# Applying an adaLN modulation after the transpose, one scalar per partition, in a linear-attention and GeGLU block

## The chip, the core and the metric

The kernel runs on one core of a Trainium2 chip, in bf16 with float32 accumulation. The core has five engines that run side by side and wait for each other through semaphores: TensorE (PE), VectorE (DVE), ScalarE (ACT), GpSimd (POOL) and SyncE (SP); SP, ACT and POOL also issue DMA transfers, each from its own queue and in program order. The metric is the device time of one launch in microseconds (us), as a median over launches.

## What is computed

One transformer block with adaptive layer norm. A conditioning vector `c` gives six vectors of 1024 entries each (shift, scale and gate, once for each half), here called `sa, ca, ga, sb, cb, gb`:

```python
mod = (_silu(c) @ w_mod).reshape(c.shape[0], 6, 1, -1)
sa, ca, ga, sb, cb, gb = (mod[:, k] for k in range(6))      # shortened
h = _layernorm(x) * (1 + ca) + sa
x = x + ga * A(h, wqkv, wo)
h = _layernorm(x) * (1 + cb) + sb
x = x + gb * B(h, w_gate, w_up, w_down)
```

`x` is 2048 tokens by 1024. `A` is linear attention with 32 heads of 32: `q, k, v = h @ wqkv`, `phi(t) = where(t > 0, t + 1, exp(t)) + 1e-6`, `kv = phi(k)^T v` and `z = sum phi(k)` for each head, `o = phi(q) kv / (phi(q) z)`, then `o @ wo`. `B` is `(gelu(h @ w_gate) * (h @ w_up)) @ w_down` with an inner width of 3584. `w_mod` is 1024 by 6144.

## The kernel before

Tokens lie in 16 tiles of 128 partitions. The kernel is written as one program order; a tracker derives every semaphore wait from overlapping memory regions, and each engine then runs its own operations in that order. Its stages are: mod vectors and layer norm 1, k and v for 16 tiles, `z` and `kv`, then q with the normalisation and the `wo` projection, layer norm 2 of the first four tiles, and a feed-forward loop over four quarters of 512 tokens.

The mod vectors are needed along the free axis of a token-major tile, the same in all 128 partitions. So each half vector is a product of the broadcast `silu(c)` (`bc`, 128 equal columns for each of 8 blocks) with a panel of `w_mod` of 1 MB:

```python
def mod_group(pan, n, defer=False, dve_copy=False):
    b = next_bank()
    items = [(bank(b), bc[:, t, :], pan[:, t, :]) for t in range(NDT)]     # 8 matmuls, 128x512
    T.mm(items)
    ...                                          # one 128x512 eviction into modt[k6], by ACT or DVE

early_evacs = []
for n in (2, 3, 0, 1):                           # ca, sa
    k = load_panel(wmod_v[:, :, n * 512:(n + 1) * 512])                    # SP queue
    early_evacs.append(mod_group(panel[k], n, defer=True, dve_copy=(n in (0, 1))))

def kv_panel_loads():
    ...                                          # four load_panel of wqkv (k, v) into the same four slots
    for k in range(4):
        T.dma("sp", mpanel[k], wmod_v[:, :, (4 + k) * 512:(5 + k) * 512], d_mpanel[k])
```

Layer norm is a pipeline of stages over tiles. In each step, every stage works on its own tile, later stages first:

```python
def s_stats(): ...      # DVE: bn_stats x2
...                     # DVE: bn_aggr, + eps; POOL: pow(-0.5); DVE: -mean * rstd
def s_hn():    T.op("act", ... a.activation(hn, x_ap, AF.Identity, bias=nm, scale=rs) ...)
def s_mod1():  T.op("dve", ... v.tensor_tensor(h, hn, ca1_t, ALU.mult) ...)    # 128x1024
def s_mod2():  T.op("dve", ... v.tensor_tensor(h, h, sa_t, ALU.add) ...)       # 128x1024
def s_tr():    T.op("sp", ... e.dma_start_transpose(dest, h) ..., ctr=dsem, inc=16)
return [s_stats, s_aggr, s_eps, s_pow, s_nm, s_hn, s_mod1, s_mod2, s_tr]

for i in range(NST):
    stages = ln_stages(xring[i % NXR1], modt[CA1], modt[SA], hT[:, i, :, :], d_trh[i], h_t)
    items.append([None] + stages + [None, (lambda i=i: kv_groups(i))])
# hooks, called after a step of the pipeline:
#   2: kv_panel_loads   6: evictions of early_evacs   m = 6..15: load_x(m)
#   8: late_mod_a: four mod_group on mpanel, then the next four w_mod panels on the SP queue
#  14: late_mod_b: four mod_group on those
```

`kv_groups(i)` holds four groups of eight 128x512 matmuls and their evictions. After the pipeline come the `z` groups (32 matmuls 128x512), the `kv` groups (128 matmuls 128x128), and a loop over pairs of tiles:

```python
for p in range(npairs + 2):
    if p < npairs:
        er_a = q_groups_and_act(ta); er_b = q_groups_and_act(tb_)
        q_minadd(er_a); q_minadd(er_b); q_ttadd(er_a); q_ttadd(er_b)     # DVE
    if 1 <= p <= npairs:
        chain_pair(2 * (p - 1), 2 * (p - 1) + 1)       # DVE: the denominators, and the scaled phi(q)
    ...                                                # wo_proj; transposes by DMA of pair p-2; numT
    if p == npairs:
        ln2_0_build()
        run_pipeline([st_[:8] for st_ in ln2_0_items])
...                                                    # the last wo_proj
for st_ in ln2_0_items:
    st_[8]()                                           # transposes into hT2, on the SP queue
```

`hT2` lies at `BIG + 120 KB`, inside the region of `oT`, which the last `wo_proj` still reads. In the feed-forward loop each quarter runs the gate and up projections (28 blocks, 448 matmuls), whose last step on each block of `AT` is a DVE operation (line 745, for the last block line 749), and then the down projection (224 matmuls):

```python
for q in range(NSC):
    ...                                                # load_panel of w_gate, w_up; gate, up, gelu -> AT
    if q + 1 < NSC:
        nxt = ln2_items(q + 1)
        run_pipeline([st_[:8] for st_ in nxt])
        pendingF = [st_[8] for st_ in nxt]
    for jj in range(4):
        for dc in range(2):
            its = [(bank(b), AT[:, jf, jj * P:(jj + 1) * P], Wd[:, jf, dc * 512:(dc + 1) * 512]) for jf in range(NFT)]
            T.mm(its)                                  # one wait for all of AT, ahead of its 28 matmuls
        ...                                            # DVE: times gb, plus x1
        T.dma("pool", out2d[j * P:(j + 1) * P, :], stg, d_o[so % NXR])
        if pendingF: pendingF.pop(0)()                 # the transpose of tile jj of the next quarter
```

Of the kernel before, what the change touches and what calls it, by code (L numbers as in the profile page):

```python
# [13 lines left out]
P = 128  # L14
# [219 lines left out]

def _build(nc, stack, A_x, A_wqkv, A_wo, B_w_gate, B_w_up, B_w_down, c, w_mod, out):
# [28 lines left out]
    cT = view(768, [P, 8], BF16)  # L264
# [3 lines left out]
    negh = view(896, [P, 1], F32)  # L268
    NLNS = 6
    def ln_small(k):  # L270
        base = 1024 + (k % NLNS) * 64
        st = view(base, [P, 12], F32)
        mv = view(base + 48, [P, 2], F32)
        rs = view(base + 56, [P, 1], F32)
        nm = view(base + 60, [P, 1], F32)
        return st, mv, rs, nm
    vi = view(2048, [P, P], I32)
# [3 lines left out]
    def den_small(k):  # L281
# [4 lines left out]
    modt = [view(4 * KB + k * 2 * KB, [P, D], BF16) for k in range(6)]  # L286
    SA, CA1, GA, SB_, CB1, GB = range(6)
# [4 lines left out]
    NHN = 2  # L292
    NHH = 3
    NHHB = 4
    hn_t = [view(TEMPS + k * 2 * KB, [P, D], BF16) for k in range(NHN)]
    h_t = [view(TEMPS + 4 * KB + k * 2 * KB, [P, D], BF16) for k in range(NHH)]
    hB_t = [view(TEMPS + 4 * KB + k * 2 * KB, [P, D], BF16) for k in range(NHHB)]
    NE1 = 4
    e1_t = [view(TEMPS + 10 * KB + k * KB, [P, 512], BF16) for k in range(NE1)]
    bc = view(TEMPS + 18 * KB, [P, NDT, P], BF16)  # L300
    xring = [view(48 * KB + k * 2 * KB, [P, D], BF16) for k in range(4)] + \
            [view(TEMPS + 14 * KB + k * 2 * KB, [P, D], BF16) for k in range(2)]
    NXR1 = 6
# [8 lines left out]
    e2_t = [view(TEMPS + 16 * KB + k * KB, [P, 512], BF16) for k in range(NE2)]  # L312
    NGT = 2
    sqz_t = [view(TEMPS + 12 * KB + k * KB, [P, 512], BF16) for k in range(NGT)]
    th_t = [view(TEMPS + 14 * KB + k * KB, [P, 512], BF16) for k in range(NGT)]
    usb_t = [view(TEMPS + 16 * KB + k * KB, [P, 512], BF16) for k in range(NGT)]
# [11 lines left out]
    hn2a_t = [view(BIG + 64 * KB + k * 2 * KB, [P, D], BF16) for k in range(2)]  # L328
    h2a_t = [view(BIG + 64 * KB + (2 + k) * 2 * KB, [P, D], BF16) for k in range(4)]
    AT = view(BIG, [P, NFT, 512], BF16)  # L330
    Wd = view(BIG + 64 * KB, [P, NFT, D], BF16)
    hT2 = view(BIG + 120 * KB, [P, 4, NDT, P], BF16)
# [23 lines left out]
    T.op("pool", lambda g: g.iota(vi, [[1, P]], base=0, channel_multiplier=-1), W=[vi])  # L356
    T.op("dve", lambda v: v.tensor_scalar(ident, vi, 0.0, None, ALU.is_equal), R=[vi], W=[ident])
    T.op("pool", lambda g: g.iota(vm.rearrange("p (a b) -> p a b", a=4), [[DH, 4], [0, DH]], base=0, channel_multiplier=-1), W=[vm])
    T.op("dve", lambda v: v.tensor_scalar(t1m, vm, 0.0, None, ALU.is_le), R=[vm], W=[t1m])
    T.op("dve", lambda v: v.scalar_tensor_tensor(mask, vm, -float(DH - 1), t1m, ALU.is_ge, ALU.mult), R=[vm, t1m], W=[mask])  # L360
    T.op("pool", lambda g: g.memset(ones, 1.0), W=[ones])
    T.op("pool", lambda g: g.memset(negh, -0.5), W=[negh])

# [15 lines left out]
    c8 = t1m[0:NDT, :]  # L379
    T.dma("act", c8, c[0].rearrange("(t p) -> t p", p=P), d_c)  # L380

# [3 lines left out]

    for i in range(NXR1):
        load_x(i, NXR1)

    pc8 = bank_bf16(7)[:, 0:NDT]
# [4 lines left out]
    T.op("dve", lambda v: v.tensor_tensor(siluT, thc, cTf, ALU.mult), R=[thc, cTf], W=[siluT])  # L394
    T.op("dve", lambda v: v.tensor_tensor(bc, ones.unsqueeze(1).to_broadcast([P, NDT, P]),
                                          siluT.unsqueeze(2).to_broadcast([P, NDT, P]), ALU.mult),
         R=[ones, siluT], W=[bc])

    def mod_group(pan, n, defer=False, dve_copy=False):
        b = next_bank()  # L400
        items = [(bank(b), bc[:, t, :], pan[:, t, :]) for t in range(NDT)]
        T.mm(items)
        k6, half = n // 2, n % 2
        dst = modt[k6][:, half * 512:(half + 1) * 512]
        if k6 in (CA1, CB1):
            ev = lambda: T.op("act", lambda a: a.activation(dst, bank(b), AF.Identity, bias=1.0, scale=1.0), R=[bank(b)], W=[dst])
        elif dve_copy:
            ev = lambda: T.op("dve", lambda v: v.tensor_copy(dst, bank(b)), R=[bank(b)], W=[dst])
        else:
            ev = lambda: T.op("act", lambda a: a.activation(dst, bank(b), AF.Copy), R=[bank(b)], W=[dst])  # L410
        if defer:
            return ev
        ev()

    early_evacs = []
    for n in (2, 3, 0, 1):
        k = load_panel(wmod_v[:, :, n * 512:(n + 1) * 512])
        early_evacs.append(mod_group(panel[k], n, defer=True, dve_copy=(n in (0, 1))))
# [7 lines left out]
    def kv_panel_loads():  # L426
        a0 = load_panel(wqkv_v[:, :, 2 * 512:3 * 512])
        a1 = load_panel(wqkv_v[:, :, 3 * 512:4 * 512])
        a2 = load_panel(wqkv_v[:, :, 4 * 512:5 * 512])
        a3 = load_panel(wqkv_v[:, :, 5 * 512:6 * 512])  # L430
        assert (a0, a1, a2, a3) == (ks0, ks1, vs0, vs1)
        for k in range(4):
            T.dma("sp", mpanel[k], wmod_v[:, :, (4 + k) * 512:(5 + k) * 512], d_mpanel[k])
# [3 lines left out]
    def ln_stages(x_ap, ca1_t, sa_t, dest, dsem, hring, hnring=None):  # L437
# [3 lines left out]
        hnring = hn_t if hnring is None else hnring  # L441
        hn = hnring[kk % len(hnring)]
        h = hring[kk % len(hring)]
# [20 lines left out]
        def s_mod1():  # L464
            T.op("dve", lambda v: v.tensor_tensor(h, hn, ca1_t, ALU.mult), R=[hn, ca1_t], W=[h])  # L465

        def s_mod2():
            T.op("dve", lambda v: v.tensor_tensor(h, h, sa_t, ALU.add), R=[h, sa_t], W=[h])  # L468

        def s_tr():  # L470
            T.op("sp", lambda e: e.dma_start_transpose(dest, h), R=[h], W=[dest], ctr=dsem, inc=16)

        return [s_stats, s_aggr, s_eps, s_pow, s_nm, s_hn, s_mod1, s_mod2, s_tr]

    def run_pipeline(stage_lists, hooks=None):
        n = len(stage_lists)
        if n == 0:
            return
        ns = max(len(x) for x in stage_lists)
        for step in range(n + ns - 1):  # L480
            for s in reversed(range(ns)):
                i = step - s
                if 0 <= i < n and s < len(stage_lists[i]) and stage_lists[i][s] is not None:
                    stage_lists[i][s]()
            if hooks and step in hooks:
                hooks[step]()
# [27 lines left out]
    for i in range(NST):  # L514
        stages = ln_stages(xring[i % NXR1], modt[CA1], modt[SA], hT[:, i, :, :], d_trh[i], h_t)

        items.append([None] + stages + [None, (lambda i=i: kv_groups(i))])
    hooks = {}
    for m in range(NXR1, NST):
        hooks[m] = (lambda m=m: load_x(m, NXR1))  # L520
    def late_mod_a():
        for k in range(4):
            mod_group(mpanel[k], 4 + k)
        for k in range(4):
            T.dma("sp", mpanel[k], wmod_v[:, :, (8 + k) * 512:(9 + k) * 512], d_mpanel[k])
    def late_mod_b():
        for k in range(4):
            mod_group(mpanel[k], 8 + k)
    def early_evac_hook():
        for ev in early_evacs:  # L530
            ev()
    prev2 = hooks.get(2)
    hooks[2] = (lambda: (prev2() if prev2 else None, kv_panel_loads()))
    prev6 = hooks.get(6)
    hooks[6] = (lambda: (prev6() if prev6 else None, early_evac_hook()))
    prev8 = hooks.get(8)
    hooks[8] = (lambda: (prev8() if prev8 else None, late_mod_a()))
    prev14 = hooks.get(14)
    hooks[14] = (lambda: (prev14() if prev14 else None, late_mod_b()))
# [7 lines left out]
    assert len({q0, q1, wo0, wo1}) == 4, (q0, q1, wo0, wo1)  # L547
    for half in range(2):
        its = [(bank(half), ones, pk[:, i, half * 512:(half + 1) * 512]) for i in range(NST)]
        T.mm(its)  # L550
    for bb in range(2):
        its = []
        for i in range(NST):
            for cc in range(4):
                c_ = bb * 4 + cc
                its.append((ps[:, (2 + bb) * 512 + cc * P:(2 + bb) * 512 + (cc + 1) * P],
                            pk[:, i, c_ * P:(c_ + 1) * P], vv[:, i, c_ * P:(c_ + 1) * P]))
        T.mm(its, W=[bank(2 + bb)])
    for half in range(2):
        T.op("act", lambda a, half=half: a.activation(zbs[:, half * 512:(half + 1) * 512], bank(half), AF.Copy),  # L560
             R=[bank(half)], W=[zbs[:, half * 512:(half + 1) * 512]])
    for bb in range(2):
        src = bank(2 + bb).rearrange("p (a b) -> p a b", a=4)
        dstk = kvbd[:, bb * 4:(bb + 1) * 4, :]
        T.op("dve", lambda v, src=src, dstk=dstk, bb=bb: v.tensor_tensor(dstk, src, mask.unsqueeze(1).to_broadcast([P, 4, P]), ALU.mult),
             R=[bank(2 + bb), mask], W=[dstk])
# [67 lines left out]
    def wo_proj(q, jjs=(0, 1, 2, 3)):  # L634
        for jj in jjs:
# [11 lines left out]
            for (ysb, cols) in grs:  # L647
                dst = x1[:, j, cols]
# [165 lines left out]
```

## Time and profile before

| what | us |
|---|---|
| median of 4 launches | 953.18 (951.58 to 953.86) |
| span of the profiled launch | 949.8 |
| PE busy | 864.5 (91%) |
| DVE busy | 480.3 (51%) |
| ACT busy | 340.6 (36%) |
| POOL busy | 45.0 (5%) |

The span is divided by the stage: the first matmul on k and v starts at 59.58 us, the feed-forward loop at 347.75 us. In the profile a line such as L209 is the helper that records every matmul, so stages are told apart by time and by shape. "Idle before" is the time an engine stood still before an instruction, with the engine or transfer that ended it last.

### The profile page before, as it was taken

To read this page: it belongs to the slowest core of one execution; us is meant where nothing else is said; L and a number is where in the kernel's file an instruction comes from. 1 tells how busy PE (TensorE), PEld (TensorE's weight loads), DVE (VectorE), ACT (ScalarE), POOL (GpSimd) and SP (SyncE) were. 2 spreads that over 40 slices of the span, in tenths; PEclk is the share of its full clock that TensorE was granted. 3 is DMA by queue.
4 is the path that set the end of the run, shared out by engine and by line. 5 is a ranking of instruction groups with operands and counts; after the bars stand their busy time and mean duration, and the time that the engine had idled before them with its cause. 6 is when DMAs were issued, how large, how long until landed. Compare 5 with 4: busy or idle time off the path is not lost.

```text
span 949.8 us, 10474 instructions
## 1 busy us (share of the span) xinstructions
PE 864.5 (91%) x4001; PEld 389.0 (41%) x4001; DVE 480.3 (51%) x955; ACT 340.6 (36%) x574; POOL 45.0 (5%) x88
## 2 busy tenths in 40 slices
PE   4349999996998659998999999899999899999898
PEld 1124444452443224443444444344444344444343
DVE  5226555248779515556515555614555713555411
ACT  2024443244463514544104554203544402444300
POOL 3011010000000100000100000100000000000000
PEclk9779999998999779999999999999999999999999
DMA  9963132503133277770623531441452170543000
GB/s 323 350 192 86 34 78 45 177 1 67 45 89 67 55 220 236 242 248 18 182 73 101 174 126 54 100 155 57 131 178 89 27 218 23 177 144 123 1 23 23
DMA packets 137329, 112.88 MB, mean 119 GB/s; under 512 B 52800, under 2 KB 130624, under 8 KB 137280
## 3 DMA queue, kind: packets, MB, share of 16 engines
q1 hardware_dynamic: 133424, 99.63, 35.2%
q0 software_dynamic: 3840, 12.59, 4.0%
q8 instruction: 32, 0.52, 0.2%
q14 instruction: 17, 0.14, 0.0%
q10 hardware_dynamic: 16, 0.00, 0.0%
HBM read 95.42 MB, written 4.19 MB: 105 GB/s over the span
## 4 chain that ended last, share of the span: by engine, by line
PE 86%; DMA 4%; DVE 4%; issue 3%; ACT 2%; SPq 2%; POOL 0%; ACTq 0%; DVEq 0%; POOLq 0%
PE ps L209 86%; DMA arena<-in_w_mod_dram 3%; SPq L197 2%; ACT arena L632 1%; DMA arena<-in_B_w_gate_dram 1%; ACT arena L462 1%; DVE arena L600 0%; ACT arena L645 0%; DMA arena<-arena 0%; DVE arena L617 0%; DVE arena L590 0%; DVE arena L749 0%; ACT arena L738 0%; DVE arena L595 0%; DVE arena L447 0%
## 5 line engine op out<-in xcount | busy, mean ns | idle before, releaser
L209 PE MATMUL ps<-arena 128*128 128x512 bf16 (+1 forms) x4000 | 864.3, 379 | 73.0 <-DMA arena<-in_w_mod_dram 18.2
L209 PEld LDWEIGHTS ps<-arena 128*128 128x128 bf16 x4000 | 388.9, 99 | 547.9 <-issue 55.4
L737 ACT ACTIVATE arena<-ps 128x512 bf16<-128x512 f32 x112 | 66.9, 597 | 201.3 <-PE ps L209 201.3
L740 DVE SCALAR_TENSOR_TENSOR arena<-ps,arena 128x512 bf16<-128x512 f32 x112 | 77.4, 691 | 117.4 <-ACT arena L738 117.4
L738 ACT ACTIVATE arena<-ps 128x512 bf16<-128x512 f32 x112 | 66.9, 597 | 127.6 <-PE ps L209 127.6
L739 DVE SCALAR_TENSOR_TENSOR arena<-arena,ps 128x512 bf16<-128x512 bf16 x112 | 77.0, 687 | 65.1 <-ACT arena L737 65.1
L770 DVE TENSOR_TENSOR arena<-ps,arena 128x512 bf16<-128x512 f32 x32 | 21.9, 690 | 134.5 <-PE ps L209 134.5
L745 DVE SCALAR_TENSOR_TENSOR arena<-arena 128x512 bf16<-128x512 bf16 x108 | 73.5, 681 | 0.0
L742 ACT ACTIVATE arena<-arena 128x512 bf16<-128x512 bf16 x112 | 69.6, 621 | 0.0
L462 ACT ACTIVATE arena<-arena 128x1024 bf16<-128x1024 bf16 x32 | 38.3, 1234 | 37.9 <-DVE arena L459 27.2
L465 DVE TENSOR_TENSOR arena<-arena 128x1024 bf16<-128x1024 bf16 x32 | 21.9, 684 | 31.1 <-DMA arena<-arena 27.4
L456 POOL TENSOR_TENSOR arena<-arena 128x1 f32<-128x1 f32 x32 | 17.7, 557 | 397.0 <-DVE arena L453 397.0
L645 ACT ACTIVATE arena<-ps 128x512 bf16<-128x512 f32 x32 | 18.8, 596 | 35.2 <-PE ps L209 35.2
L579 ACT ACTIVATE arena<-ps 128x512 bf16<-128x512 f32 x32 | 19.3, 604 | 27.9 <-PE ps L209 25.8
L197 POOL DMA_DIRECT2D arena<-in_A_x_dram x32 | 17.8, 558 | 229.7 <-DVE arena L649 149.2
L502 ACT ACTIVATE arena<-ps 128x512 bf16<-128x512 f32 x16 | 9.6, 597 | 37.9 <-PE ps L209 37.9
L500 ACT ACTIVATE arena<-ps 128x512 bf16<-128x512 f32 x16 | 9.6, 597 | 36.2 <-PE ps L209 36.2
L468 DVE TENSOR_TENSOR arena<-arena 128x1024 bf16<-128x1024 bf16 x32 | 22.0, 687 | 0.3
L446 DVE BATCH_NORM_STATS2 arena<-arena 128x6 f32<-128x512 bf16 x32 | 20.8, 651 | 2.4 <-DMA arena<-in_A_x_dram 2.4
L197 POOL DMA_DIRECT2D out_dram<-arena x16 | 8.8, 549 | 275.2 <-DVE arena L774 275.2
L447 DVE BATCH_NORM_STATS2 arena<-arena 128x6 f32<-128x512 bf16 x32 | 21.6, 676 | 0.0
L586 DVE TENSOR_SCALAR arena<-arena 128x512 bf16<-128x512 bf16 x32 | 8.6, 290 | 24.1 <-ACT arena L579 24.0
(48 smaller groups left out, 237.7 us busy)
## 6 DMA issues: line engine op xcount, KB each, us to landing
arena<-in_B_w_gate_dram SPq DMA_DIRECT2D x28, 1024.0 KB, 5.4
arena<-in_B_w_up_dram SPq DMA_DIRECT2D x28, 1024.0 KB, 7.5
arena<-in_w_mod_dram SPq DMA_DIRECT2D x12, 1024.0 KB, 11.8
arena<-in_A_x_dram POOLq DMA_DIRECT2D x32, 256.0 KB, 3.2
arena<-in_B_w_down_dram SPq DMA_DIRECT2D x7, 1024.0 KB, 10.2
arena<-in_A_wqkv_dram SPq DMA_DIRECT2D x6, 1024.0 KB, 9.0
out_dram<-arena POOLq DMA_DIRECT2D x16, 256.0 KB, 2.3
arena<-in_A_wo_dram SPq DMA_DIRECT2D x2, 1024.0 KB, 8.7
```

What stands on the lines that cost most here:

```text
L197: return self.op(eng, lambda e: e.dma_start(out_ap, in_ap), R=R, W=W, ctr=ctr, inc=16)
L209: ins = t.matmul(o, l, r, start=(fs and i == 0), stop=(ls and i == n - 1))
L462: T.op("act", lambda a: a.activation(hn, x_ap, AF.Identity, bias=nm, scale=rs), R=[x_ap, nm, rs], W=[hn])
L465: T.op("dve", lambda v: v.tensor_tensor(h, hn, ca1_t, ALU.mult), R=[hn, ca1_t], W=[h])
L468: T.op("dve", lambda v: v.tensor_tensor(h, h, sa_t, ALU.add), R=[h, sa_t], W=[h])
L737: T.op("act", lambda a, sqz=sqz, bg=bg: a.activation(sqz, bank(bg), AF.Square, scale=math.sqrt(GELU_A)), R=[bank(bg)], W=[sqz])
L738: T.op("act", lambda a, usb=usb, bu=bu: a.activation(usb, bank(bu), AF.Copy), R=[bank(bu)], W=[usb])
L739: T.op("dve", lambda v, sqz=sqz, bg=bg: v.scalar_tensor_tensor(sqz, sqz, 1.0, bank(bg), ALU.add, ALU.mult), R=[sqz, bank(bg)], W=[sqz])
L740: T.op("dve", lambda v, dstA=dstA, usb=usb, bg=bg: v.scalar_tensor_tensor(dstA, bank(bg), 0.5, usb, ALU.mult, ALU.mult), R=[bank(bg), usb] ...
L742: T.op("act", lambda a, th=th, sqz=sqz: a.activation(th, sqz, AF.Tanh, scale=GELU_C), R=[sqz], W=[th])
L745: T.op("dve", lambda v, pd=pd, pth=pth: v.scalar_tensor_tensor(pd, pth, 1.0, pd, ALU.add, ALU.mult), R=[pth, pd], W=[pd])
L770: T.op("dve", lambda v, dst=dst, b=b, cols=cols: v.tensor_tensor(dst, bank(b), modt[GB][:, cols], ALU.mult), R=[bank(b), modt[GB][:, cols] ...
```

## The change

The modulation moves from before the transpose to after it. In the transposed tile, feature runs along the partitions, so scale and shift are one scalar for each partition and block of 128 features, and a broadcast copy of the vector isn't needed. With that:

- **Vectors.** `ca`, `sa`, `cb`, `sb` become columns: for each block of 128 features, eight matmuls with a 128x128 block of the `w_mod` panel as weights and one column of `silu(c)` as the moving operand (`modT_vec`). Only `ga` and `gb` stay broadcast (`bc_group`).
- **Modulation.** The two DVE operations on 128x1024 go; eight GpSimd operations on 128x128, in place on the transposed tile, come (`mod_eng` is "pool" in every call).
- **Loads.** The panels for the other eight half vectors are no longer loaded in the first stages on the SP queue: four are loaded from the POOL queue at step 12 of the pipeline, four after the first have been used, and their matmuls stand between the k, v stage and the q stage. The ring of `x` tiles grows from 6 to 8.
- **Order.** `chain_pair` comes ahead of the min and add of the same step. The transposes of the first four tiles of layer norm 2 go to an `hT2` at 8 KB, where no later reader of `oT` is in the way.
- **Down projection.** The first group is cut after 24 of its 28 matmuls, so that only the last four wait for the last blocks of `AT`.

The core of the diff (views renamed, banks named by a counter and constants issued later are left out):

```diff
-    hT2 = view(BIG + 120 * KB, [P, 4, NDT, P], BF16)
+    hT2 = view(8 * KB, [P, 4, NDT, P], BF16)
...
+    for n in (2, 3, 0, 1):
+        load_panel(wmod_v[:, :, n * 512:(n + 1) * 512])
+    def modT_vec(pan_lo, pan_hi, dstT, plus1, b):
+        for t in range(NDT):
+            pan = pan_lo if t < 4 else pan_hi
+            c0 = (t % 4) * P
+            items = [(bank(b)[:, t:t + 1], pan[:, kt, c0:c0 + P], siluTb[:, kt:kt + 1]) for kt in range(NDT)]
+            T.mm(items, W=[bank(b)[:, t:t + 1]])
+        ...                                            # one ACT eviction of 128x8
+    modT_vec(panel[pan_ca0], panel[pan_ca1], ca1T, True, next_bank())
+    modT_vec(panel[pan_sa0], panel[pan_sa1], saT, False, next_bank())
...
-        def s_mod1(): ...
-        def s_mod2(): ...
         def s_tr():
-            T.op("sp", lambda e: e.dma_start_transpose(dest, h), R=[h], W=[dest], ctr=dsem, inc=16)
-        return [s_stats, s_aggr, s_eps, s_pow, s_nm, s_hn, s_mod1, s_mod2, s_tr]
+            T.op("sp", lambda e: e.dma_start_transpose(dest, hn), R=[hn], W=[dest], ctr=dsem, inc=16)
+        def s_mod():
+            for t in range(NDT):
+                blk = dest[:, t, :]
+                T.op("pool", lambda g, blk=blk, t=t: g.tensor_scalar(blk, blk, c1T[:, t:t + 1], sT[:, t:t + 1], ALU.mult, ALU.add),
+                     R=[blk, c1T, sT], W=[blk])
+        return [s_stats, s_aggr, s_eps, s_pow, s_nm, s_hn, s_tr, s_mod]
...
-    hooks[8], hooks[14]: late_mod_a, late_mod_b
+    add_hook(1, kv_panel_loads)
+    def mpanel_round1():
+        for k, n in enumerate((4, 5, 6, 7)):
+            T.dma("pool", mpanel[k], wmod_v[:, :, n * 512:(n + 1) * 512], d_mpanel[k])
+    add_hook(12, mpanel_round1)
...
+    bc_group(mpanel[0], modGA[:, 0:512])
+    bc_group(mpanel[1], modGA[:, 512:1024])
+    modT_vec(mpanel[2], mpanel[3], sbT, False, next_bank())
+    for k, n in enumerate((8, 9, 10, 11)):
+        T.dma("pool", mpanel[k], wmod_v[:, :, n * 512:(n + 1) * 512], d_mpanel[k])
     ...                                               # the z and kv groups
+    modT_vec(mpanel[0], mpanel[1], cb1T, True, next_bank())
+    bc_group(mpanel[2], modGB[:, 0:512])
+    bc_group(mpanel[3], modGB[:, 512:1024])
...
         if p < npairs:
             er_a = q_groups_and_act(ta)
             er_b = q_groups_and_act(tb_)
+        if 1 <= p <= npairs:
+            chain_pair(2 * (p - 1), 2 * (p - 1) + 1)
+        if er_a is not None:
             q_minadd(er_a)
             ...
-        if 1 <= p <= npairs:
-            chain_pair(2 * (p - 1), 2 * (p - 1) + 1)
...
     for st_ in ln2_0_items:
-        st_[8]()
+        st_[6]()
+    for st_ in ln2_0_items:
+        st_[7]()
...
-                T.mm(its)
+                if jj == 0 and dc == 0:
+                    T.mm(its[:24], last_stop=False)
+                    T.mm(its[24:], first_start=False)
+                else:
+                    T.mm(its)
...
+            if pendingF:
+                ftr, fmod = pendingF.pop(0)
+                ftr()
+                fmod()
             T.dma("pool", out2d[j * P:(j + 1) * P, :], stg, d_o[so % NXR])
-            if pendingF:
-                pendingF.pop(0)()
```

## The prediction

> **What bounds the kernel now.** TensorE is busy 91% of the span, so a gain has to come from its idle 85 us or from work taken off it. I first read the stretches of matmuls in order of time (start, length, engine, line, shape, count, and in brackets the idle time before and what ended it):
>
> ```profile
> 19.12 1.90 PE L209 MATMUL ps<-arena 128*128 128x512 bf16 x8 [0.97 <-DMA arena<-in_w_mod_dram]
> 36.21 5.12 PE L209 MATMUL ps<-arena 128*128 128x512 bf16 x16 [15.19 <-DMA arena<-in_w_mod_dram]
> ...
> 59.58 119.33 PE L209 MATMUL ps<-arena 128*128 128x512 bf16 x544 [12.44 <-issue]
> 180.12 41.84 PE L209 MATMUL ps<-arena 128*128 128x512 bf16 x288 [1.21 <-DVE arena L510]
> 229.63 62.66 PE L209 MATMUL ps<-arena 128*128 128x512 bf16 x280 [7.67 <-DMA arena<-arena]
> ...
> 321.70 16.09 PE L209 MATMUL ps<-arena 128*128 128x512 bf16 x64 [3.29 <-ACT arena L632]
> 347.75 99.58 PE L209 MATMUL ps<-arena 128*128 128x512 bf16 x448 [9.96 <-DMA arena<-in_B_w_gate_dram]
> 449.94 145.21 PE L209 MATMUL ps<-arena 128*128 128x512 bf16 x672 [2.62 <-DVE arena L749]
> 597.77 146.90 PE L209 MATMUL ps<-arena 128*128 128x512 bf16 x672 [2.62 <-DVE arena L749]
> 747.29 145.21 PE L209 MATMUL ps<-arena 128*128 128x512 bf16 x672 [2.62 <-DVE arena L749]
> 895.12 50.21 PE L209 MATMUL ps<-arena 128*128 128x512 bf16 x224 [2.62 <-DVE arena L749]
> ```
>
> The reader is to see four kinds of holes: the start, until 59.58; one ahead of the first numerator matmuls, 7.67; one at the door of the feed-forward loop, 9.96; and four of 2.62 ahead of the down projections. Inside the long stretches a 128x512 matmul takes 145.21 / 672 = 0.216 us. Then the queue of SyncE, which shows why the start is so long:
>
> ```profile
> 0.75 8.66 SPq L197 DMA_DIRECT2D arena<-in_w_mod_dram  x4
> 13.99 8.56 SPq L197 DMA_DIRECT2D arena<-in_A_wqkv_dram  x4
> 22.60 25.55 SPq L197 DMA_DIRECT2D arena<-in_w_mod_dram  x8
> 48.20 11.60 SPq L471 DMA_TRANSPOSE arena<-arena  x3
> ```
>
> Sixteen panels of 1 MB go ahead of the first transpose. Eight of them (the third line) aren't needed by k and v, but the first transpose is issued only at 48.20 and lands 11.3 us later, where the median of all such transposes is 3.3. The first k, v matmul at 59.58 waits for it. The stage windows give 337 GB/s over the first 60 us: the start is bound by transfers.
>
> Last, the rows of GpSimd (busy, mean ns, idle before), as it takes over the modulation:
>
> ```profile
> L456 POOL TENSOR_TENSOR arena<-arena 128x1 f32<-128x1 f32 x32 | 17.7, 557 | 397.0 <-DVE arena L453 397.0
> L361 POOL MEMSET arena<- 128x128 bf16 x1 | 0.3, 274 | 0.0
> L358 POOL IOTA arena<- 128x128 int32 x1 | 0.2, 236 | 0.0
> L362 POOL MEMSET arena<- 128x1 f32 x1 | 0.2, 173 | 0.0
> ```
>
> It is nearly free, and a 128x128 operation there costs about a quarter of a microsecond. No row shows the operation that the change uses.
>
> [...] In the `kv` groups (128x128) the trace has 22 matmuls and 20 weight loads in each of two windows of 1 us: about 0.05 us a pair. I take that for the new matmuls with one column.
>
> **Part 1, the start.** Eight panels of w_mod leave the queue ahead of the first transpose. What is left are 8 panels of 1.05 MB and some nine x tiles of 0.26 MB: 10.8 MB at 337 GB/s is 32 us, plus 2 for the first issue. The first transpose is behind them and lands at about 36. Eight GpSimd operations of 0.35 us add 2.8. First k, v matmul at 39 instead of 59.6: 20.6 gained. The column products need 32 pairs for each panel, no more time than the 8 wide matmuls that freed a panel before, and lie beside the transfers.
>
> **Part 2, k and v.** This stretch held 512 matmuls of k, v and 32 of late_mod_b: 119.3 us. Without the 32 it is 112.3: 7.0 gained. Sixteen tiles in 112.3 us are 7.0 us a tile. GpSimd has to keep up with 8 x 0.35 + 0.56 (pow) + 0.56 (issue of an x tile) = 3.9 us. It does, with room up to (7.0 - 1.1) / 8 = 0.74 us an operation. VectorE loses 2 x 0.68 us a tile here (44 us in the whole kernel), but it had slack (65 busy of 119), so nothing is gained by that.
>
> **Part 3, between k, v and q.** Before, from 178.9 to 194.4: 15.5 us. The two broadcast products of `ga` cover the old gap of 1.2. Added are 32 wide matmuls, 6.9 us, and 128 narrow ones at 0.05, 6.4 us; I add 1 for a late panel, since four panels on the POOL queue, four on the SP queue and four x tiles, 9.4 MB, 28 us at 337 GB/s, fall in this window. 28.6 in all: 13.1 lost. So q starts at 39 + 112.3 + 28.6 = 180 instead of 194.4: 14.5 gained by parts 1 to 3.
>
> **Part 4, the first q pairs.** Before, VectorE waited from about 203.5 for the second pair's evictions before it began the first denominator chain at 210.4. With the chain first it may begin some 6 us sooner. But then the first min and add of the second pair waits behind a chain of 6.6 us, and with it the exp of the third pair, whose buffers it holds (a ring of four). That gives back part of it. I book 2 of the 7.67.
>
> **Part 5, the door of the feed-forward loop.** Before, the transposes waited on the SP queue for the end of the last wo_proj (337.8), and the gate panel waited behind them. With `hT2` elsewhere they go when the normalised tiles are there (315.8), the panels behind them. GpSimd then has 32 operations, behind the x tiles whose last issue was at 321.1: 32 x 0.35 = 11 us, to 332, ahead of the 337.8. The hole of 9.96 closes, and with it the slow matmuls after it: 99.58 us for 448, where 0.216 each would be 96.8. Of these 12.8 I book 10.
>
> **Part 6, the down projections.** The 24 matmuls that no longer wait last 5.2 us, the hole 2.62: all four close, 10.5. Two of the four stretches after a hole were longer by 1.7 to 1.8 us than at 0.216 each; I book 1.5 for that. 12 gained. In the loop GpSimd's last tile is modulated after the third output is issued, with a quarter of the down projection, 12 us, left for 2.8 us of work.
>
> **Sum.** 14.5 + 2 + 10 + 12 = 38.5. 953.2 - 38.5 = 914.7, so 915.
>
> **The rivals.** *GpSimd becomes the bound.* For it: the operation has no row, it is in place with two scalar columns[...]. Against: the rows above. At 0.6 us k, v still fits and part 5 leaves a gap of some 3: 918. At 1.0 us a tile takes 9.1, the k, v stage 146 instead of 112, and 32 operations end at 353 instead of 338: part 5 gives nothing and costs about 5; sum 953 - 38.5 + 34 + 25 = 963 with the smaller losses left out, slower than before. *The moved panels come late.* A panel is 1024 rows of 1 KB on the POOL queue, where issuing 128 rows of 2 KB took 0.56; if the issue grows with the rows, four of them hold GpSimd for some 18 us at step 12 and the modulations behind them wait, and the second round comes too late for `cb`. GpSimd is then some two tiles (14 us) ahead, so most is hidden: plus 3 to 12, 918 to 927. *The start is bound by something else.* If the chain c, silu, column products, rather than the panels, sets the time, k, v starts at 45 and not 39: 921. *TensorE work isn't saved.* True: 64 wide matmuls (13.8 us) leave and 256 narrow ones (12.8) come; all the gain is holes, so it can't go beyond the holes counted.
>
> **Range and chances.** The closing of the four small holes (10.5) and most of the start rest on the order of queues alone, and those two are over 20 us. The middle rivals, alone or two together, give 918 to 935. The wins that I booked low (parts 4 and 5) could give 8 more with a faster start: 900. I take 900 to 936. Only slow GpSimd makes it a loss, and I give it about one in sixteen; 2% faster is 934. Faster 0.85, within 2% 0.1, slower 0.05.
>
> **What would show it right or wrong.** Right: the first k, v matmul near 39, its stretch near 112 without breaks; a GpSimd row of 128x128 at 0.3 to 0.45 us, 256 times; narrow matmuls at 0.05 us; no releaser L749 before a down projection; the gap before the gate matmuls under 3. Wrong: TensorE waiting on GpSimd in the k, v stage (an operation over 0.74 us), a wait on w_mod between k, v and q, or a start beyond 46.

## The result, and the profile after

The changed kernel takes 897.79 us, the kernel before 952.61 on the same chip: a ratio of 0.942 (95% interval 0.941 to 0.943). The change saves 54.8 us, where 38.5 was predicted, and the time lies below the range of 900 to 936. The profiled launches differ by 949.8 - 897.1 = 52.7 us; the stage sums below are of these. The other 2 us lie in which launches were profiled: that of the kernel before took 951.58, 1.0 under the median, and that of the changed kernel 898.99, 1.2 over it.

The stretches of matmuls in order of time, as shown before:

```profile
17.60 1.01 PE L209 MATMUL ps<-arena 128*128 128x1 bf16 x32 [2.00 <-DMA arena<-in_w_mod_dram]
20.61 1.01 PE L209 MATMUL ps<-arena 128*128 128x1 bf16 x32 [2.00 <-DMA arena<-in_w_mod_dram]
38.96 136.05 PE L209 MATMUL ps<-arena 128*128 128x512 bf16 x824 [17.34 <-POOL arena L460]
175.53 29.51 PE L209 MATMUL ps<-arena 128*128 128x512 bf16 x136 [0.52 <-DMA arena<-in_w_mod_dram]
205.52 61.19 PE L209 MATMUL ps<-arena 128*128 128x512 bf16 x280 [0.48 <-DMA arena<-arena]
269.59 16.54 PE L209 MATMUL ps<-arena 128*128 128x512 bf16 x68 [2.88 <-ACT arena L631]
290.76 2.06 PE L209 MATMUL ps<-arena 128*128 128x512 bf16 x4 [4.63 <-ACT arena L644]
296.11 596.52 PE L209 MATMUL ps<-arena 128*128 128x512 bf16 x2752 [3.29 <-ACT arena L631]
```

All holes that the change aimed at are gone: the one ahead of the numerators (205.52) is 0.48, and from 296.11 to the end of the last matmul there is one stretch without a break, where before were the 9.96 at the door and four of 2.62. The holes of 2.88, 4.63 and 3.29, which the change doesn't touch, are as before. The start is at 38.96. It is put down to GpSimd, but GpSimd's first modulation itself waited for the first transpose, as its queue shows:

```profile
35.40 3.46 POOL L460 TENSOR_SCALAR arena<-arena 128x128 bf16<-128x128 bf16 x8 [11.26 <-DMA arena<-arena]
...
65.54 3.54 POOL L197 DMA_DIRECT2D arena<-in_w_mod_dram  x4
69.12 3.95 POOL L460 TENSOR_SCALAR arena<-arena 128x128 bf16<-128x128 bf16 x8
...
121.72 3.58 POOL L460 TENSOR_SCALAR arena<-arena 128x128 bf16<-128x128 bf16 x8 [3.34 <-DMA arena<-arena]
...
294.78 16.58 POOL L460 TENSOR_SCALAR arena<-arena 128x128 bf16<-128x128 bf16 x32
```

A tile costs 3.46 to 4.1 us (0.43 to 0.51 an operation), late in the k, v stage GpSimd waits over 3 us for each next transpose, and four panels of 1 MB are issued in 3.54 us. At the door it ends at 311.36, just ahead of the first gate matmuls at 312.2. The stage windows (start and end, length, busy time and count of PE, PEld, DVE, ACT and POOL in this order, where PEld is TensorE's loading of weights, then granted clock, DMA share, GB/s) give the account:

```profile
38.96:152.55 113.59, 113.59 (x513) 50.95 (x514) 54.83 (x140) 48.25 (x76) 69.43 (x143) 1.00 0.37 92
152.55:177.40 24.85, 24.33 (x322) 16.54 (x320) 1.36 (x3) 2.15 (x5) 5.75 (x8) 1.00 0.99 336
177.40:205.50 28.10, 27.64 (x129) 12.36 (x127) 22.68 (x53) 16.63 (x32) 0.00 (x0) 1.00 0.20 38
205.50:296.10 90.60, 79.53 (x352) 34.58 (x352) 72.71 (x178) 52.78 (x96) 9.93 (x20) 0.95 0.39 79
296.10:312.20 16.10, 16.09 (x64) 6.88 (x65) 5.59 (x13) 4.18 (x7) 15.26 (x29) 0.85 0.64 215
312.20:409.00 96.80, 96.80 (x450) 43.83 (x448) 54.53 (x84) 47.43 (x83) 0.00 (x0) 1.00 0.59 195
```

| stage | before, us | after, us | saved | predicted |
|---|---|---|---|---|
| start, to the first k, v matmul | 59.6 | 39.0 | 20.6 | 20.6 |
| k and v | 119.3 | 113.6 | 5.7 | 7.0 |
| between k, v and q | 15.5 | 24.85 | -9.35 | -13.1 |
| q begins, to the first numerator matmul | 35.2 | 28.1 | 7.1 | 2 |
| from there to the last wo_proj | 92.1 | 90.6 | 1.5 | 0 |
| last wo_proj, the door, first gate and up | 125.65 | 112.9 | 12.75 | 10 |
| the rest | 502.45 | 488.1 | 14.35 | 12 |
| sum | 949.8 | 897.15 | 52.65 | 38.5 |

### The profile page after: what moved, and what is told of

It reads as the page before. It is cut to its first block, busy times and chain, and to the rows that moved or that the text cites. A ratio compares the mean times of both kernels' runs of the same rounds, so it can differ in the third digit from the quotient of the medians.

```text
span 897.1 us, 11065 instructions
## 1 busy us (share of the span) xinstructions
PE 845.8 (94%) x4193; PEld 388.1 (43%) x4193; DVE 444.1 (49%) x890; ACT 336.7 (38%) x572; POOL 170.4 (19%) x352
## 3 DMA queue, kind: packets, MB, share of 16 engines
q1 hardware_dynamic: 125104, 91.24, 35.4%
## 4 chain that ended last, share of the span: by engine, by line
PE 86%; issue 5%; DMA 4%; DVE 2%; ACT 2%; POOL 1%; SPq 0%; POOLq 0%; ACTq 0%; DVEq 0%
PE ps L209 86%; DMA arena<-in_w_mod_dram 4%; DVE arena L599 1%; DVE arena L616 0%; ACT arena L631 0%; DVE arena L589 0%; ACT arena L451 0%; POOL arena L460 0%; ACT arena L644 0%; SPq L197 0%; DVE arena L594 0%; ACT arena L578 0%; POOL arena L445 0%; ACT arena L579 0%; DVE arena L585 0%
## 5 line engine op out<-in xcount | busy, mean ns | idle before, releaser
L209 PE MATMUL ps<-arena 128*128 128x512 bf16 (+2 forms) x4192 | 845.6, 363 | 40.4 <-POOL arena L460 17.3
L738 ACT ACTIVATE arena<-ps 128x512 bf16<-128x512 f32 x112 | 66.9, 597 | 179.5 <-PE ps L209 179.5
L460 POOL TENSOR_SCALAR arena<-arena 128x128 bf16<-128x128 bf16 x256 | 118.3, 474 | 43.6 <-DMA arena<-arena 42.9
L739 ACT ACTIVATE arena<-ps 128x512 bf16<-128x512 f32 x112 | 66.9, 597 | 126.5 <-PE ps L209 126.5
L644 ACT ACTIVATE arena<-ps 128x512 bf16<-128x512 f32 x32 | 18.7, 595 | 35.4 <-PE ps L209 35.4
L647 DVE TENSOR_TENSOR arena<-arena 128x512 bf16<-128x512 bf16 x32 | 13.4, 430 | 28.2 <-ACT arena L644 28.1
L578 ACT ACTIVATE arena<-ps 128x512 bf16<-128x512 f32 x32 | 19.5, 609 | 19.4 <-PE ps L209 11.3
L496 ACT ACTIVATE arena<-ps 128x512 bf16<-128x512 f32 x16 | 9.6, 597 | 39.2 <-PE ps L209 39.2
L494 ACT ACTIVATE arena<-ps 128x512 bf16<-128x512 f32 x16 | 9.6, 597 | 38.2 <-PE ps L209 38.2
L579 ACT ACTIVATE arena<-ps 128x512 bf16<-128x512 f32 x32 | 19.4, 608 | 0.0
## 6 DMA issues: line engine op xcount, KB each, us to landing
arena<-in_w_mod_dram POOLq DMA_DIRECT2D x8, 1024.0 KB, 12.1
arena<-in_w_mod_dram SPq DMA_DIRECT2D x4, 1024.0 KB, 14.5
```

The lines of the kernel that those rows point to most:

```text
L209: ins = t.matmul(o, l, r, start=(fs and i == 0), stop=(ls and i == n - 1))
L460: T.op("pool", lambda g, blk=blk, t=t: g.tensor_scalar(blk, blk, c1T[:, t:t + 1], sT[:, t:t + 1], ALU.mult, ALU.add), R=[blk, c1T, sT], W= ...
L738: T.op("act", lambda a, sqz=sqz, bg=bg: a.activation(sqz, bank(bg), AF.Square, scale=math.sqrt(GELU_A)), R=[bank(bg)], W=[sqz])
L739: T.op("act", lambda a, usb=usb, bu=bu: a.activation(usb, bank(bu), AF.Copy), R=[bank(bu)], W=[usb])
```

## The experiments

Each time is a median, beside the kernel before at 951.7 to 951.8 in the same group of runs; "changed kernel" is the 897.8 above, which was taken beside 952.6, so that a difference of 1 us to it says nothing.

**The down projection whole again.**

```diff
-                if jj == 0 and dc == 0:
-                    T.mm(its[:24], last_stop=False)
-                    T.mm(its[24:], first_start=False)
-                else:
-                    T.mm(its)
+                T.mm(its)
```

> The changed kernel (897.8) with the first down-projection group whole again, so that all its 28 matmuls wait for the last block of AT. Theory 1: each of the four holes of 2.62 comes back, and after some holes the first matmuls run slowly again, as in the kernel before (1.7 and 1.8 us in two of four): 897.8 + 10.5 + 3.5 = about 912. Theory 2: the slow matmuls came from something else than the hole, and only the holes come back: 908. If the hole were hidden elsewhere by now: 898 to 900.

Measured 911.82, ratio to the kernel before 0.958 (0.956 to 0.960): 14.0 slower than the changed kernel. Its matmul stretches:

```profile
408.91 145.21 PE L209 MATMUL ps<-arena 128*128 128x512 bf16 x672 [2.61 <-DVE arena L750]
556.74 146.90 PE L209 MATMUL ps<-arena 128*128 128x512 bf16 x672 [2.62 <-DVE arena L750]
706.25 146.90 PE L209 MATMUL ps<-arena 128*128 128x512 bf16 x672 [2.62 <-DVE arena L750]
855.77 48.52 PE L209 MATMUL ps<-arena 128*128 128x512 bf16 x224 [2.62 <-DVE arena L750]
```

All four holes are back, and two of the stretches are again 1.7 us longer for the same 672 matmuls. Theory 1 holds: the cut is worth its holes (10.5) and what follows them (3.4). The weight loads after such a hole in the kernel before, from 1.7 us after its end on, show what that is:

```profile
599.52 0.15 PEld L209 LDWEIGHTS ps<-arena 128*128 128x128 bf16 x1 [0.28 <-issue]
599.94 0.15 PEld L209 LDWEIGHTS ps<-arena 128*128 128x128 bf16 x1 [0.28 <-issue]
600.37 0.15 PEld L209 LDWEIGHTS ps<-arena 128*128 128x128 bf16 x1 [0.28 <-issue]
```

They follow each other at 0.43 us, twice the 0.216 of a full stretch: about eight such steps are the 1.7. The granted clock was 0.57 from 599.4 to 603.0 us, and 1.00 from 449.9 to 456.0, after a hole that no slow matmuls follow; but at the start of the changed kernel the same steps of 0.43 stand beside a granted clock of 1.00 (38.96 to 44.9 us). So what slows them is not shown. Slow matmuls don't come after every hole: two of four here.

**The old order in the pair loop.**

```diff
-        if 1 <= p <= npairs:
-            chain_pair(2 * (p - 1), 2 * (p - 1) + 1)
         if er_a is not None:
             q_minadd(er_a)
             ...                                       # q_minadd and q_ttadd of both tiles
+        if 1 <= p <= npairs:
+            chain_pair(2 * (p - 1), 2 * (p - 1) + 1)
```

> The changed kernel with the old order in the pair loop: min and add of the pair first, then the denominator chain. Theory 1: the chain-first order closes the hole ahead of the first numerator matmuls and gives nothing back later: the hole of 7.7 comes back, about 905. Theory 2, as I predicted: most of it is given back by evictions that wait behind the chain: about 900. If the removal of the modulation from VectorE closed that hole: 898.

Measured 906.65, ratio 0.952 (0.951 to 0.954): 8.9 slower than the changed kernel.

```profile
174.41 29.51 PE L209 MATMUL ps<-arena 128*128 128x512 bf16 x136 [0.99 <-DMA arena<-in_w_mod_dram]
211.28 62.83 PE L209 MATMUL ps<-arena 128*128 128x512 bf16 x280 [7.37 <-DMA arena<-arena]
```

The hole is back at 7.37, and the stretch after it is 1.6 longer than the 61.19 of the changed kernel. So the order closes it, and nearly nothing is given back.

**The new order alone, in the kernel before.**

```diff
+        if 1 <= p <= npairs:
+            chain_pair(2 * (p - 1), 2 * (p - 1) + 1)
+        if p < npairs:
             q_minadd(er_a)
             ...                                       # q_minadd and q_ttadd of both tiles
-        if 1 <= p <= npairs:
-            chain_pair(2 * (p - 1), 2 * (p - 1) + 1)
```

> The kernel before with nothing but the order of the pair loop changed: the denominator chain ahead of the min and add. Theory 1: the order alone closes the hole of 7.7 and gives nothing back: 952 - 7 to 9, about 944. Theory 2, as I predicted for this part: 950. Theory 3: it needs a VectorE freed of the modulation: 952.

Measured 942.58, ratio 0.990 (0.988 to 0.991): 9.1 faster than the kernel before.

```profile
222.21 1.67 PE L209 MATMUL ps<-arena 128*128 128x512 bf16 x7 [0.46 <-DMA arena<-arena]
```

The order alone closes the hole, as theory 1 says; theory 3, that a VectorE freed of the modulation was needed, falls.

**More buffers for exp**, to see what the waiting evictions cost.

```diff
-    NE2 = 4
-    e2_t = [view(TEMPS + 16 * KB + k * KB, [P, 512], BF16) for k in range(NE2)]
+    NE2 = 8
+    e2_t = [view(TEMPS + 16 * KB + k * KB, [P, 512], BF16) for k in range(4)] + \
+           [view(12 * KB + k * KB, [P, 512], BF16) for k in range(4)]
```

> The changed kernel with eight exp buffers in the pair loop instead of four. My prediction took the chain-first order to be paid for by the exp of the third pair, which waits for a buffer behind the chain (in the trace ScalarE does wait 2.1 and 4.0 us there). Theory 1: that wait lies beside the matmuls of the next pairs and costs TensorE nothing: 897 to 898, the same. Theory 2: it costs what I predicted, and more buffers win it: 892 to 895.

Measured 897.6, ratio 0.943 (0.942 to 0.944): the same. Two lines of ScalarE's waits in the changed kernel (in total, times, longest):

```profile
ACT arena L578 <- PE ps L209: 11.3, 18, 1.1
ACT arena L578 <- DVE arena L589: 7.0, 3, 4.0
```

With eight buffers the second line is gone from the list, and the first is longer:

```profile
ACT arena L579 <- PE ps L209: 17.0, 27, 1.1
```

So the waits that I charged for are real, 7.0 us of them, but ScalarE had that much to spare: what it waits for a buffer in one kernel, it mostly waits for TensorE in the other.

**hT2 at its old place.**

```diff
-    hT2 = view(8 * KB, [P, 4, NDT, P], BF16)
+    hT2 = view(BIG + 120 * KB, [P, 4, NDT, P], BF16)
```

> The changed kernel with hT2 at its old place, where the last wo_proj still reads oT. Theory 1: the place is what hides GpSimd's modulation at the door of the feed-forward loop. The transposes wait for the end of wo_proj, land 3.3 us later, and 32 GpSimd operations, 16.6 us in the trace of the changed kernel, follow in the open, with the gate panel behind the transposes meanwhile: a hole of about 22 us and slow matmuls after it, 897.8 + 24 = about 922. Theory 2: the place only frees the panel loads, and GpSimd works tile by tile beside them: about 908. Theory 3: the place doesn't matter: 898.

Measured 914.1, ratio 0.960 (0.958 to 0.962): 16.3 slower than the changed kernel, between theories 1 and 2. GpSimd's and then TensorE's queue at the door (the view begins at 296 us, so that its first line has only the last five of the first tile's eight operations):

```profile
295.66 2.16 POOL L460 TENSOR_SCALAR arena<-arena 128x128 bf16<-128x128 bf16 x5
314.98 10.37 POOL L460 TENSOR_SCALAR arena<-arena 128x128 bf16<-128x128 bf16 x24 [17.16 <-DMA arena<-arena]
```

```profile
325.50 582.73 PE L209 MATMUL ps<-arena 128*128 128x512 bf16 x2688 [13.87 <-POOL arena L460]
```

The mechanism is that of theory 1, with a smaller size: the first tile doesn't overlap what the last wo_proj reads and went early, so 24 operations and not 32 stand in the open, and they are faster, 10.37 / 24 = 0.43 us, than the 16.58 / 32 = 0.52 of the changed kernel. TensorE ended at 311.63, the last transposes landed 3.35 later, GpSimd worked for 10.37 and TensorE began 0.15 after it: the hole of 13.87. The new place is thus worth more than the hole of 9.96 that it closed: without it, GpSimd's work would lie open.

**Four w_mod panels back in the start.**

```diff
         assert tuple(a) == (ks0, ks1, vs0, vs1)
+        for k, n in enumerate((4, 5, 6, 7)):
+            T.dma("sp", mpanel[k], wmod_v[:, :, n * 512:(n + 1) * 512], d_mpe[k])
...
-    add_hook(12, mpanel_round1)
```

> The changed kernel with the first four of the moved w_mod panels (ga, sb) loaded again on the SP queue right behind the k, v panels, ahead of the first transpose; the other four stay where they are. Theory 1: the start is bound by transfers in the order of the queue. 4 x 1.05 MB at 337 GB/s are 12.4 us: first k, v matmul at 51.4 instead of 39.0, time about 910. Theory 2: the start is bound by the chain from c to the column products and layer norm, and the transfers hide: start at 39 to 41, time 898 to 900.

Measured 910.35, ratio 0.956 (0.955 to 0.958): 12.6 slower, and the k, v matmuls start at

```profile
51.09 135.36 PE L209 MATMUL ps<-arena 128*128 128x512 bf16 x824 [29.55 <-POOL arena L463]
```

Theory 1 holds to 0.3 us: the start is set by the bytes ahead of the first transpose.

**GpSimd's work doubled.**

```diff
+        def s_mod_twice():
+            s_mod()
+            for t in range(NDT):
+                ...                                    # the same block again, times 1, plus 0
-        return [..., s_tr, s_mod]
+        return [..., s_tr, s_mod_twice]
```

> The changed kernel with every GpSimd modulation followed by a second pass over the same eight blocks (times 1, plus 0), so that GpSimd's work is doubled and nothing else changes. In the trace of the changed kernel an operation takes 0.43 to 0.52 us, a tile with its pow and x issue some 4.9. Theory 1: GpSimd is hidden with the room I worked out (7.0 us a tile in the k, v stage), and doubled it passes it: 16 x 0.45 + 1.2 = 8.4 a tile, the k, v stage about 20 us longer, the start 3.5 later, and 64 operations at the door end some 16 us after the last wo_proj; 897.8 + 42 = about 940. Theory 2: GpSimd is far from any bound and the double work hides too: 898 to 903.

Measured 936.41, ratio 0.984 (0.982 to 0.985): 38.6 slower than the changed kernel. TensorE now waits on GpSimd tile by tile:

```profile
67.62 7.07 PE L209 MATMUL ps<-arena 128*128 128x512 bf16 x31 [1.58 <-POOL arena L474]
76.54 7.07 PE L209 MATMUL ps<-arena 128*128 128x512 bf16 x31 [1.84 <-POOL arena L474]
```

A tile's period there is 76.54 - 67.62 = 8.9 us, where 7.07 is work. This is the turn the prediction named: GpSimd is hidden only as long as a tile takes it under some 7 us.

**The modulation on ScalarE.**

```diff
-    def ln_stages(..., hnring, mod_eng="pool"):
+    def ln_stages(..., hnring, mod_eng="act"):
```

> The changed kernel with the modulation on ScalarE (scale and bias columns of an activation) instead of GpSimd. Estimate for an operation, from 0.62 us for 128x512 and 0.18 to 0.21 for 128x8 in the trace: 0.25 to 0.3 us. Theory 1: what counts is a queue of its own. In the k, v stage ScalarE has room (48 of 114 us busy), but at the door its 32 operations stand in its queue behind the last wo_proj evictions: a hole of 8 to 10 and slow matmuls after it, about 909. Theory 2: a faster engine is simply better, about 895. Theory 3: no difference, 898.

Measured 914.04, ratio 0.959 (0.958 to 0.961). The k, v stage is whole, as expected, and the door has a hole that ends with line 463, the modulation:

```profile
325.90 581.87 PE L209 MATMUL ps<-arena 128*128 128x512 bf16 x2668 [12.98 <-ACT arena L463]
```

An operation took 0.48 us, and 100.5 / 256 = 0.39 us of ScalarE's time as neighbours overlap, not the 0.25 to 0.3 of my estimate, so the hole is larger than the expected 8 to 10.

**The modulation on VectorE.**

```diff
-                    T.op("pool", lambda g, blk=blk, t=t: g.tensor_scalar(
+                    T.op("dve", lambda g, blk=blk, t=t: g.tensor_scalar(
```

> The changed kernel with the modulation on VectorE, still after the transpose. Estimate for an operation, from 0.29 us for a 128x512 tensor_scalar: 0.12 to 0.17 us, a third of GpSimd's. Theory 1: what counts is a queue of its own. VectorE's queue puts the operations behind the last wo_proj additions (hole of some 6.5 at the door) and, for the last tile of each quarter, behind the output of the whole down projection (three holes of some 3.5), with slow matmuls after each: about 915 to 920. Theory 2: the faster operation wins: about 895.

Measured 922.41, ratio 0.969 (0.967 to 0.971).

```profile
320.07 146.66 PE L209 MATMUL ps<-arena 128*128 128x512 bf16 x667 [9.04 <-DVE arena L460]
469.96 146.81 PE L209 MATMUL ps<-arena 128*128 128x512 bf16 x667 [3.24 <-DVE arena L460]
620.02 146.88 PE L209 MATMUL ps<-arena 128*128 128x512 bf16 x667 [3.24 <-DVE arena L460]
770.13 146.90 PE L209 MATMUL ps<-arena 128*128 128x512 bf16 x667 [3.24 <-DVE arena L460]
```

The holes are where theory 1 put them, at the door and after each of three down projections. VectorE is the quickest of the three for this operation (59.5 / 256 = 0.23 us of its time each, where ScalarE took 0.39 and GpSimd 118.3 / 256 = 0.46) and makes the slowest kernel of the three: its queue stands in the way, not its speed.

**Layer norm 2 of the first tiles earlier.**

```diff
-        if p == npairs:
+        if p == npairs - 2:
             ln2_0_build()
```

> The changed kernel with layer norm 2 of the first four tiles two pair steps earlier (p == npairs - 2 instead of p == npairs); its transposes and modulation stay where they are. In the changed kernel TensorE still waits 4.6 us for an eviction (line 644) that stands behind the four normalisations on ScalarE. Theory 1: earlier there is slack, TensorE is busy without a break: the 4.6 us go, about 893. Theory 2: the work then delays the evictions of the full stretch and the hole only moves: about 898.

Measured 894.73, ratio 0.940 (0.938 to 0.941): 3.1 faster than the changed kernel.

```profile
272.83 17.75 PE L209 MATMUL ps<-arena 128*128 128x512 bf16 x71 [3.51 <-ACT arena L631]
293.46 2.20 PE L209 MATMUL ps<-arena 128*128 128x512 bf16 x6 [2.88 <-ACT arena L631]
295.88 593.42 PE L209 MATMUL ps<-arena 128*128 128x512 bf16 x2724 [0.22 <-issue]
```

The 4.63 is gone, but some small holes (0.58 twice, 0.33, 0.22) stand in the stretches before and after: partly won, partly moved.

**Two transposes ahead of the k, v panels.**

```diff
-    modT_vec(panel[pan_sa0], panel[pan_sa1], saT, False, next_bank())
+    sa_evict = modT_vec(panel[pan_sa0], panel[pan_sa1], saT, False, next_bank(), defer=True)
...
-    add_hook(1, kv_panel_loads)
+    add_hook(6, sa_evict)
+    add_hook(7, kv_panel_loads)
```

> The changed kernel with the k, v panels issued at step 7 instead of step 1 of the layer norm pipeline, so that two transposes stand ahead of them in the SP queue, and the eviction of sa at step 6, so that it doesn't hold up the first normalisations on ScalarE. No transfer is added or removed. Theory 1: the start is the sum of the transfers up to the last k, v panel, and the first transpose and its modulation only have to be moved beside it: matmuls start near 25, the fourth panel lands near 35, the first k, v tile ends near 37 instead of 46; about 890. Theory 2: it is the last panel alone and nothing is won by the order: 897.

Measured 891.06, ratio 0.936 (0.934 to 0.937): 6.7 faster than the changed kernel.

```profile
27.82 3.57 PE L209 MATMUL ps<-arena 128*128 128x512 bf16 x8 [6.15 <-POOL arena L447]
34.39 134.37 PE L209 MATMUL ps<-arena 128*128 128x512 bf16 x816 [2.99 <-DMA arena<-in_A_wqkv_dram]
```

Now TensorE waits for the k, v panels themselves (34.39). The modulation of the first tile, 3.5 us, no longer comes behind them, and the first eight matmuls are done by then. The 6.15 ahead of those is put down to line 447, a step of a later tile's layer norm that they don't need; in the next run the same wait is put down to a k, v panel.

**Both of these** (the last two diffs together).

> The two changes of e8_ln2_at_6 and e9_transposes_first together. They lie in different stages; if both gains stand they add: 897.8 - 3 - 8 = about 887. If the order of the start wins nothing: 894.7, as e8_ln2_at_6.

Measured 889.48, ratio 0.934 (0.933 to 0.935). The fastest version here, but only 1.6 better than the one before it. The reason is on its door:

```profile
303.37 580.32 PE L209 MATMUL ps<-arena 128*128 128x512 bf16 x2688 [1.39 <-POOL arena L462]
```

With a hole closed ahead of it, TensorE arrives at the door before GpSimd has done its 32 operations.

## Why the prediction was wrong

The direction of each part was right, and so was the mechanism of all but part 4, which charged a wait that costs TensorE nothing. The sum was too small: 38.5 predicted, 52.7 in the profiled launches. The error of 14.2 lies in these terms.

- **Part 1, right.** First k, v matmul at 39 predicted, 38.96 measured; the run with four of the eight panels put back moved it by 12.1 for a predicted 12.4. That 39 was met to the decimal is luck: the transpose was in by 35.4, not 36, and the eight operations took 3.46, not 2.8. The 0.35 us for one of them, here and in parts 2 and 5, was an estimate of mine that no row of the trace before shows; the nearest there are 0.23 to 0.27 for a memset or an iota of 128x128.
- **Part 2, 1.3 too high.** The stage took 113.6, not 112.3. GpSimd had the room that was worked out: the doubled run shows the turn. The 1.3 is not GpSimd's. The stretch that begins at 38.96 lasted 136.05 in this launch and 134.54 for the same 824 matmuls in the run with the whole group. It begins with weight loads at the slow step of 0.43 us, until 44.9 here, at a granted clock of 1.00. The 1.51 between the two launches is what seven such steps cost over 0.216, so by an estimate from these numbers they ended near 41.9 there. What sets the number of slow steps stays open.
- **Part 3, 3.75 too pessimistic.** The term that was mis-sized is the narrow matmul. I took 0.05 us from pairs with 128 columns; with one column 32 pairs take 1.01 us, 0.031 each. 128 of them at 0.019 less are 2.4 us. The late panel cost 0.5, not 1; the last 0.9 of the 3.75 is not accounted for. The 256 narrow matmuls thus took some 8 us, not the 12.8 that the rival on TensorE's work set against the 13.8 that leave. Issuing a panel from GpSimd took 0.90 us, where a rival had feared some 4.5.
- **Part 4, the step that failed: 5.1 too low.** I wrote that the exp of the third pair, waiting behind the chain, "gives back part of it", and booked 2 of 7.67. The stage gave 7.1. The order undone costs 8.9, the order alone in the kernel before gives 9.1, and more exp buffers change nothing. The wait exists, but ScalarE had slack in that stretch, and TensorE's next matmuls didn't depend on it yet: from 177.4 to 205.5 it was busy for 27.64 of 28.10 us. I charged a wait without asking who waits for the waiter. With it, the next stretch became 1.5 shorter, 61.19 for 280 matmuls where it was 62.66 behind the hole of 7.67 (and 62.83 behind the 7.37 of the run with the old order); that term was missing from the sum.
- **Part 5, 2.75 too low.** All of the 12.8 was won; I booked 10 out of caution. GpSimd's operation was slower at the door than estimated, 0.52 and not 0.35, and 0.47 on the mean of the kernel, but it ended at 311.4 against 312.2. The margin that I took to be 6 us was 0.8.
- **Part 6, 2.4 too low.** The holes gave 10.5 and the slow matmuls after them 3.4 or more, of which I booked 1.5. The run with the whole group measures the part at 14.0.

The three discounts together (parts 4, 5 and 6) are 10.2 of the 14.2. Those of parts 5 and 6 were caution, which belongs in the range and not in the middle. The lower end of 900 lay only 4 below a plain sum of the holes and the slow matmuls after them: 14.5 + 7.67 + 12.8 + 10.5 + 3.5 = 49, or 904.

One sum of the prediction doesn't come out. For a GpSimd operation of 1.0 us it has 953 - 38.5 + 34 + 25 = 963; as written that is 973.5, and with what its own words give for part 5 (10 not won, 5 lost) the last term is 15 and the result 963.5.

No run keeps the modulation ahead of the transpose and makes the rest of the change, so what the move is worth by itself, apart from the loads that it lets wait, is not shown.

## What to carry to other kernels

A wait on an engine that isn't the bound is a cost only if the bounding engine waits for it in turn; follow the wait to its last waiter before it is put in a sum. Before a short operation is given to an engine, see what stands ahead of it in that engine's queue: here the slowest engine with an empty queue beat the fastest with a full one, by 25 us. When a hole on TensorE closes, count the slow matmuls that may follow it too (1.7 us after two holes of four here), and find which engine's slack has become the next margin.

## What the runs showed of the hardware

- A 128x128 bf16 tensor_scalar with two scalar columns on GpSimd took 0.43 us with VectorE idle (24 operations, hT2 at its old place) and 0.52 on the mean beside VectorE's operations on two SBUF tensors (32 at the door of the changed kernel). One by one in the changed kernel's trace: 142 operations that met no VectorE instruction lasted 0.44 us, 56 that met only casts, statistics and other operations with at most one tensor from SBUF 0.45, and 29 that met a tensor_tensor with both inputs in SBUF 0.67, the longest of them 1.22; the other 29, beside its tensor_scalar, 0.48. At the door 24 of the 32 lasted 0.44 to 0.45. What makes an operation longer beside such a tensor_tensor wasn't tried apart; DMA traffic alone doesn't, as the 24 operations at 0.43 ran beside 302 GB/s. The estimate of 0.35 in the prediction was too low by a quarter of the 0.47 that it took on the mean.
- A matmul with one column and its own 128x128 weights took 0.031 us a pair, also right after a wait of 2 us; with 128 columns the pair took about 0.05.
